# A list-scheduled attention kernel: where its transposes stand, and the paces its plan reckons with

## The chip, the cores and the metric

The kernel runs on one core of a Trainium2 chip. The metric is the device time of one execution in microseconds. Engine names are those of the profile: PE is TensorE (matmuls), PEld its weight loads, DVE VectorE, ACT ScalarE, POOL GpSimd, SP the engine whose queue issues all DMAs. A matmul multiplies a stationary operand, loaded beforehand by a weight load, with a moving operand that streams past it; its result lands in one of eight PSUM banks of 128 x 512 words.

## What is computed

Two attention layers A and B work on the same input and are mixed by a gate per token. Each layer has 32 heads of 20 features and goes through the 2048 tokens in 4 segments of 512: causal softmax attention inside the segment, and a memory `M`, `z` that sums earlier segments.

```python
def layer(x, wq, wk, wv, wo, beta):                 # 2048 x 640, H = 32, Dh = 20
    for s in range(4):                              # segments of 512 tokens
        p = softmax(qs @ ks.T * scale + mask)
        a_dot = p @ vs
        a_mem = (phi(qs) @ M) / (phi(qs) @ z + 1e-6)
        o = g * a_mem + (1 - g) * a_dot             # g = sigmoid(beta), per head
        M = M + phi(ks).T @ vs;  z = z + phi(ks).sum(tokens)
    return concat(o) @ wo
gate = sigmoid((x * gate_w).sum(-1))
return gate * layer_A + (1 - gate) * layer_B
...
phi(t) = t + 1 where t > 0, else exp(t)
```

## The kernel before

**Stages.** A step `t` (0 to 7) is one layer of one segment. Its projections q, k, v and o run in split precision: each operand is taken apart into a high and a low part, and three products are summed (`product`, matmuls of L695: 15 per 128 output features and half, with 512 or 320 columns). `qk_finish` and `hi_lo_out` split the results again and send them through DRAM into score operands (`qst`, `kst`), four heads at a time. Such a group of four heads is a slot `i`, 64 in all. A slot has S-units (`s_unit`, L1127: scores by query block, of which DVE takes the row maximum, L1114), a transpose of those maxima (`mrow_unit`, L1152), their copy into spare rows of `qst` by DMA, T-units (`t_unit`, L1217: scores by key block with the maximum already subtracted; ACT takes the exponential, L1209, POOL masks the diagonal, L1210), and one P·V group (`pv_unit`, L1237). `fin_unit` transposes the P·V result back and weighs it; `o_transpose` transposes the output for the o product; `back_unit` transposes phi(k) for the memory's update (`update_unit`, L883); `mem_unit` (L805) reads the memory. The last output products of the last step are full-array matmuls (L1056).

**Two halves.** Matmuls of 64 rows or fewer use one half of the array. The program keeps two sequences, `lane[0]` and `lane[1]`, and writes for each half its own matmuls; P·V and a few other groups use all 128 rows and join the halves (`whole`, `pv_unit`). A unit from `split_unit` has its lower-row part and its upper-row part; one half starts it (`firsts`), the other adds its own part later into the same bank (`seconds`). A transpose unit has four transposes for each half (`turn`, L843), the maxima's one.

**The order.** The whole program is laid out by a planner that runs when the kernel is built. It keeps a clock `clk`, plans when each instruction ends from given paces (`mm(n)` for a matmul of n columns, the numbers in `put(engine, duration, ...)`, `DONE` for signalling), and emits an instruction on an engine when the plan has it start. `op` and `next_start` reckon when a half can begin its next matmul: not before the one in front has streamed, and not before the weights are there, which can be fetched only once the one in front has begun (`lead`). Nothing of this runs on the chip; there the engines follow their own order and wait for each other by semaphores.

`lane_step` picks the next matmul of a half: first blocks of S- and T-units (`lane_ops`), then a second half that is ready, then the unit in progress; with none, `start_unit` starts a delayed unit (`start_late`, from the list `late` that `later` fills) or goes on with the projections (`fill`). Slots are spread over time by `marks`, and `RULES` gives each slot its order of S and T units and five numbers: `span`, `calm` (planned load of DVE above which low-priority delayed units are kept back), `lag` (time between the first half's last matmul and the second half's first), `room` and `hold`.

Of the kernel before, what the change touches and what calls it, by code (L numbers as in the profile page):

```python
# [15 lines left out]
AF = mybir.ActivationFunctionType  # L16
# [26 lines left out]
def tile_gated_mix_infini_attn(  # L43
# [50 lines left out]
        3: "TSTSTSTSTS 0.978 2.38 0.24 8 0.0",  # L94
        4: "TSTSTSTSTS 1.010 2.38 0.30 8 0.0",
        5: "TSSTTSSTTS 1.010 2.38 0.30 8 0.0",
        6: "TSTSTSTSTS 0.931 2.38 0.30 6 0.0",
        7: "TTSTSTSTSS 1.031 2.38 0.30 8 0.0",
        8: "TSTSTSTSTS 1.009 2.38 0.30 8 0.9",
        9: "STSTSTSTST 0.982 2.95 0.37 8 0.0",  # L100
        10: "TSTSTSTSTS 1.044 2.38 0.30 8 0.0",
        11: "TTSSTTSSTS 1.010 2.92 0.32 8 0.0",
        12: "TSTSTSTSTS 0.935 2.22 0.35 6 3.4",
        13: "TSTSTSTSTS 1.010 2.67 0.30 8 1.6",
        14: "TSTSTSTSTS 1.010 2.38 0.30 8 0.0",
        15: "TSTSTSTSTS 1.022 1.56 0.26 8 0.0",
        16: "TSTSTSTSTS 0.947 2.38 0.30 8 0.0",
        17: "TSTSTSTSTS 1.056 2.38 0.30 8 0.0",
        18: "TSTSTSTSTS 0.946 2.38 0.31 8 0.0",
        19: "TSTSTSTSTS 0.954 2.38 0.30 8 0.0",  # L110
        20: "STTSTSSTST 1.010 2.38 0.39 8 0.0",
        21: "TSTSTSTSTS 1.005 2.81 0.30 8 0.0",
        22: "TSTSTSTSTS 1.048 1.51 0.36 8 0.0",
        23: "TSSTTSSTTS 1.025 2.74 0.30 8 0.0",
        24: "TSTSTSTSTS 0.968 3.16 0.30 8 3.5",
        25: "TSTTSSTSTS 1.010 1.69 0.22 8 0.0",
        26: "TSTSTSTSTS 1.010 2.38 0.30 8 0.0",
        27: "TSTSTSTSTS 1.055 1.45 0.32 8 0.0",
        28: "TSTSTSTSTS 0.927 2.38 0.22 4 0.0",
        29: "TTSTSTSTSS 1.010 3.28 0.30 8 0.0",  # L120
        30: "TSTSTSTSTS 0.905 2.38 0.35 8 0.3",
        31: "TSTSTSTSTS 1.022 2.38 0.23 8 0.0",
        32: "TSTSTSTSTS 0.939 3.80 0.26 8 0.0",
        33: "TSTSTSTSTS 1.048 2.75 0.30 8 0.0",
        34: "TSTSTSTSTS 0.901 2.38 0.38 8 0.0",
        35: "TSTSTSTSTS 0.973 2.38 0.30 6 0.0",
        36: "STTSTSSTST 1.010 2.38 0.36 8 0.0",
# [1467 lines left out]
```

## Time and profile before

| | |
|---|---|
| median of 3 runs | 1045.03 us (1043.71 to 1046.25) |
| the profiled execution | 1042.96 us, span 1041.3 us |
| granted TensorE clock, mean | 0.999 |
| projections, L695, of the chain of waits | 52% |
| P·V, L1237 | 13% |
| T-units L1217, S-units L1127 | 7% each |
| transposes L843 | 4% |

The span runs from the first to the last instruction; the profiled execution's own time has 1.7 us more around it. A busy PE is not a PE at its peak: a matmul's recorded duration contains its way through the array, and any wait for its weights. So two matmuls are compared by the distance between their ends on the same half, and the two halves overlap in the timeline. A line of the timeline merges neighbours of one kind: it has the start of the first, the time from there to the end of the last, and the count.

### The profile page before, as it was taken

The page shows a single profiled execution, that of the slowest core. Times are in us where ns is not written, and L with a number is a line of the kernel's source. Part 1 is how long each engine was busy: PE and PEld are TensorE (multiplying, and loading weights), DVE is VectorE, ACT ScalarE, POOL GpSimd, SP SyncE. Part 2 cuts the span into 40 slices and gives each one's busy share as a digit, 9 for nine tenths or more (in the row PEclk, how much of TensorE's full clock was granted, in tenths as well). Part 3 has the DMA queues.
Part 4 walks back from the last instruction along what each step waited for, and adds up shares of the span by engine and source line. Part 5 has one row for each costly group of instructions (what it writes and reads, how often), then busy time and mean ns, then how long its engine had stood idle before and what let it go on. Part 6 is the DMA issues. An engine that isn't in the chain of part 4 may idle for free.

```text
span 1041.3 us, 31917 instructions
## 1 busy us (share of the span) xinstructions
PE 1031.3 (99%) x11780; PEld 870.4 (84%) x11780; DVE 760.8 (73%) x2725; ACT 660.2 (63%) x1337; POOL 581.7 (56%) x1043
## 2 busy tenths in 40 slices
PE   9999999999999999999999999999999999999998
PEld 7987888888888878888798887988879888888776
DVE  4787877558776688775877768976577767978844
ACT  5476666667564685665756557576574746757572
POOL 3565654556454674747736457375773635736462
PEclk9999999999999999999999999999999999999999
DMA  8997677658575486755858458674576855858432
GB/s 269 295 302 187 205 214 215 191 161 269 136 251 157 137 291 187 226 177 151 262 146 255 134 153 279 202 244 136 163 226 204 266 152 182 264 148 242 117 117 76
DMA packets 110028, 207.97 MB, mean 200 GB/s; under 512 B 12464, under 2 KB 16560, under 8 KB 109872
## 3 DMA queue, kind: packets, MB, share of 16 engines
q1 hardware_dynamic: 109872, 205.93, 65.2%
q8 instruction: 93, 1.52, 0.6%
q14 instruction: 63, 0.52, 0.2%
HBM read 131.43 MB, written 73.40 MB: 197 GB/s over the span
## 4 chain that ended last, share of the span: by engine, by line
PE 89%; DVE 3%; DMA 3%; ACT 2%; issue 1%; POOL 1%; SPq 0%; ACTq 0%; DVEq 0%; POOLq 0%
PE bank L695 52%; PE bank L1237 13%; PE bank L1217 7%; PE bank L1127 7%; PE bank L843 4%; PE bank L883 3%; PE bank L805 2%; DVE bank L1114 1%; DMA kd<-row 1%; DMA wst<-in_x_dram 1%; PE bank L741 1%; PE bank L1152 0%; POOL wl L524 0%; DMA row<-in_xT_dram 0%; PE bank L1056 0%
## 5 line engine op out<-in xcount | busy, mean ns | idle before, releaser
L1114 DVE CUSTOM_DVE_ANT_0 bank<-bank,tri 128x384 f32<-128x384 f32 (+3 forms) x1024 | 474.0, 522 | 146.3 <-PE bank L1127 117.6
L695 PE MATMUL bank<-row,wh 64*128 64x512 f32 x2308 | 535.2, 407 | 0.0
L1209 ACT ACTIVATE p<-bank 128x512 f32<-128x512 f32 x606 | 333.3, 599 | 155.6 <-PE bank L1217 124.5
L1210 POOL TENSOR_SCALAR_AFFINE_SELECT p<-p 128x256 f32<-128x256 f32 (+1 forms) x606 | 218.7, 370 | 243.9 <-ACT p L1209 233.4
L695 PEld LDWEIGHTS bank<-row,wh 64*128 64x128 f32 x2308 | 325.9, 185 | 12.4 <-issue 2.6
L695 PE MATMUL bank<-row,wl 64*128 64x512 f32 x1154 | 302.5, 402 | 0.0
L524 POOL TENSOR_TENSOR wl<-wst,wh 128x640 fp32r<-128x640 f32 x115 | 179.6, 1566 | 74.7 <-ACT wh L522 73.1
L695 PE MATMUL bank<-wvh,row 64*128 64x320 f32 x1280 | 202.4, 317 | 0.1
L1127 PE MATMUL bank<-kst,qst 60*128 60x384 f32 (+3 forms) x1024 | 176.9, 321 | 0.9 <-DVE O L1304 0.4
L695 PEld LDWEIGHTS bank<-row,wl 64*128 64x128 f32 x1154 | 170.4, 186 | 4.8 <-issue 0.6
L1217 PE MATMUL bank<-qst,kst 62*128 62x384 f32 (+3 forms) x1024 | 172.8, 323 | 1.1 <-DVE mw L819 0.7
L695 PEld LDWEIGHTS bank<-wvh,row 64*128 64x128 f32 x1280 | 161.1, 185 | 2.9 <-issue 1.4
L1237 PE MATMUL bank<-p,vst 128*32 128x128 f32 (+2 forms) x1980 | 148.3, 430 | 0.0
L1114 DVE DVE_READ_ACCUMULATOR2_ANT mx<- 128x1 f32 x1024 | 146.7, 143 | 0.0
L1217 PEld LDWEIGHTS bank<-qst,kst 62*128 62x128 f32 x1024 | 125.3, 185 | 17.1 <-DVE mx L1114 4.6
L1127 PEld LDWEIGHTS bank<-kst,qst 60*128 60x128 f32 x1024 | 125.1, 185 | 13.0 <-DVE mx L1114 2.9
L1237 PEld LDWEIGHTS bank<-p,vst 128*32 128x32 f32 x1980 | 59.4, 109 | 87.6 <-issue 68.3
L695 PE MATMUL bank<-wvl,row 64*128 64x320 f32 x640 | 113.3, 312 | 0.0
L522 ACT CAST wh<-wst 128x640 fp32r<-128x640 f32 x119 | 86.5, 736 | 34.5 <-PE bank L695 27.6
L695 PEld LDWEIGHTS bank<-wvl,row 64*128 64x128 f32 x640 | 88.7, 185 | 0.7 <-issue 0.4
L499 POOL TENSOR_TENSOR wvl<-wst,wvh 128x640 fp32r<-128x640 f32 (+1 forms) x48 | 63.9, 1336 | 21.3 <-ACT wvh L496 21.0
L664 DVE TENSOR_TENSOR row<-bank,row 128x512 fp32r<-128x512 f32 x80 | 54.4, 688 | 29.1 <-ACT row L652 15.3
(100 smaller groups left out, 1224.1 us busy)
## 6 DMA issues: line engine op xcount, KB each, us to landing
qd<-row SPq DMA_DIRECT2D x120, 256.0 KB
kd<-row SPq DMA_DIRECT2D x120, 256.0 KB
qst<-qd SPq DMA_DIRECT2D x128, 240.0 KB
kst<-kd SPq DMA_DIRECT2D x128, 240.0 KB
wst<-in_a_wq_dram SPq DMA_DIRECT2D x20, 320.0 KB
wst<-in_a_wk_dram SPq DMA_DIRECT2D x20, 320.0 KB
wst<-in_b_wq_dram SPq DMA_DIRECT2D x20, 320.0 KB
wst<-in_b_wk_dram SPq DMA_DIRECT2D x20, 320.0 KB
```

Of the source, the lines that this page charges most:

```text
L499: put("G", 0.77 * n, lambda: nc.gpsimd.tensor_tensor(out=wl[:, a:b, :], in0=w3, in1=r32(wh[:, a:b, :]), op=ALU.subtract), end, prio=4)
L522: put("A", 0.625, lambda: nc.scalar.copy(wh, w3), lambda: put(lo_eng, lo_cost, lambda: lo.tensor_tensor(out=wl, in0=w3, in1=r32(wh), op=AL ...
L524: lambda: lo.tensor_tensor(out=wl, in0=w3, in1=r32(wh), op=ALU.subtract), end, prio=3), prio=6)
L664: put("D", 0.605, lambda: nc.vector.tensor_tensor(out=lo, in0=src, in1=r32(hi), op=ALU.subtract), out, prio=1)
L695: return nc.tensor.matmul(bank_of, lhsT=w[ROWS[half]], rhs=x_[ROWS[half]], start=start, stop=stop)
L843: return nc.tensor.transpose(px[:, n, r], block(n)[r], ident[r, r])
L1114: put("D", w / 960.0 + 0.085, lambda: nc.vector.tensor_tensor_reduce(out=sc[:, off:off + w], in0=sc[:, off:off + w], in1=tri[:, L - w:], s ...
L1127: lane_ops[half].append((mm(w), lambda pair=pair, qb=qb, off=off, w=w, r=r, sc=sc: nc.tensor.matmul(sc[:, off:off + w], lhsT=q[r, pair, P ...
L1209: put("A", 0.483, lambda: nc.scalar.activation(pt, sc, AF.Exp, scale=SCALE), lambda: (bank.give(sc), put("G", 0.15 + 0.105 * len(todo), la ...
L1210: "G", 0.15 + 0.105 * len(todo), lambda: nc.gpsimd.affine_select(out=blocks, in_=blocks, pattern=[[0, len(todo)], [1, P]], base=0, channel ...
L1217: lane_ops[half].append((mm(w), lambda pair=pair, kb=kb, off=off, w=w, r=r, sc=sc: nc.tensor.matmul(sc[:, off:off + w], lhsT=k[r, pair, P ...
L1237: nc.tensor.matmul(po[32 * j:32 * j + 32, P * kb:], lhsT=vst[t % 2][:, kb, h * E1:h * E1 + 32], rhs=pts[i, n, f][0][:, off:off + w], start ...
```

## The change

- `RULES` has new entries for most slots and a sixth number, `wait`. Slots that have no entry keep the values of the slot in front.
- `mm(n)` counts 0.008 + 0.000438 n us where it counted 0.0004333 n. The two ACT reads of a projection's bank count 0.475 and 0.487 (0.483), the exponential behind the relu 0.525 (0.56). The row maximum counts 0.02 more, and what follows it is planned 0.05 later.
- In `hi_lo_phi`, the DVE operation `low_part` is planned only when both ACT operations that read the bank are through.
- `op` notes in `quick[half]` whether the matmul just placed is shorter than the load of the next weights; P·V sets it for both halves.
- Delayed units that are transposes carry the time at which they were asked for (`later(..., turns=True)`); memory and update units do not. `start_late` takes a transpose unit only once it is `wait` old. With `only=True` it takes transpose units at once, whatever their age. `lane_step` asks so right behind a quick matmul, also inside a product in progress, and `start_unit` does when nothing else is there.
- A transpose unit that one half has begun is finished without a break; the second half's part is taken when the second half has a quick matmul behind it, or `wait` later.

```diff
@@ -88,79 +88,74 @@
     RULES = {
-        0: "TTSTSTSTSS 1.055 2.80 0.30 8 0.0",
-        1: "TSSTTSSTTS 1.010 2.38 0.33 4 0.0",
-        2: "STTSTSSTST 1.010 1.93 0.39 8 0.0",
...
+        0: "TSTSTSTSTS 0.906 2.61 0.29 8 0.0 1.6",
+        1: "STSTSTSTST 1.025 2.27 0.25 8 0.0 1.6",
+        2: "TSTSTSTSTS 1.060 2.14 0.30 8 0.0 0.29",
...
     }
     rule = {}
     DONE = {"A": 0.17, "D": 0.135, "G": 0.11, "S": 0.0}
     FULL, LEADT = 0.113, 0.056
     def mm(n):
-        return 0.008 + n * 0.0004333, FULL, 1
+        return 0.008 + n * 0.000438, FULL, 1
     def quad4(n):
         return 0.0027 + n / 1200.0, FULL, 2
@@ -239,6 +234,7 @@
     begun = [0.0, 0.0]
     fetched = [0.0]
     joined = [True]
+    quick = [True, True]
     def whole(dur, emit):
         if not joined[0]:
@@ -269,6 +265,7 @@
         for _ in range(parts - 1):
             start += max(stream, 0.003 + lead)
         begun[half], lane[half] = start, start + stream
+        quick[half] = lead + 0.003 > stream
         advance(now[0])
         return emit()
@@ -622,8 +619,8 @@
     late = []
-    def later(prio, cost, ok, fn):
-        late.append((prio, next(seq), cost, ok, fn))
+    def later(prio, cost, ok, fn, turns=True):
+        late.append((prio, next(seq), clk[0] if turns else None, ok, fn))
         late.sort(key=lambda x: x[:2])
@@ -648,19 +645,19 @@
                     "D", 0.605, lambda: nc.vector.tensor_tensor(out=r32(y), in0=pp, in1=r32(y), op=ALU.min), end, prio=1), prio=1)
             read = then_all(2, over)
-            hi_lo_out(pp, hi, lo, dst, m, read, then)
-            put("A", 0.483, lambda: nc.scalar.activation(r32(y), pp, AF.Exp), read, prio=1)
+            low = hi_lo_out(pp, hi, lo, dst, m, read, then, 2)
+            put("A", 0.487, lambda: nc.scalar.activation(r32(y), pp, AF.Exp), lambda: (low(), read()), prio=1)
         else:
             both = then_all(2, lambda: put("D", 0.605, lambda: nc.vector.scalar_tensor_tensor(
                 out=r32(y), in0=pp, scalar=0.0, in1=r32(y), op0=ALU.max, op1=ALU.add), end, prio=1))
-            hi_lo_out(pp, hi, lo, dst, m, both, then)
-            put("A", 0.483, lambda: nc.scalar.activation(r32(y), pp, AF.Relu, scale=-1.0), lambda: put(
-                "A", 0.56, lambda: nc.scalar.activation(r32(y), r32(y), AF.Exp, scale=-1.0), both, prio=1), prio=1)
-
-    def hi_lo_out(src, hi, lo, dst, m, read, then):
+            low = hi_lo_out(pp, hi, lo, dst, m, both, then, 2)
+            put("A", 0.487, lambda: nc.scalar.activation(r32(y), pp, AF.Relu, scale=-1.0), lambda: (low(), put(
+                "A", 0.525, lambda: nc.scalar.activation(r32(y), r32(y), AF.Exp, scale=-1.0), both, prio=1)), prio=1)
+
+    def hi_lo_out(src, hi, lo, dst, m, read, then, reads=1):
         is_q = any(dst is x for x in qd)
-        def low():
+        def low_part():
             put("D", 0.605, lambda: nc.vector.tensor_tensor(out=lo, in0=src, in1=r32(hi), op=ALU.subtract), out, prio=1)
         def out():
@@ -677,7 +674,9 @@
                     dma(0.7, lambda c=c, part_=part_: nc.sync.dma_start(
                         out=r32(dst[P * m:P * (m + 1), c, :]), in_=r32(part_)), one, prio=-1)
-        put("A", 0.483, lambda: nc.scalar.copy(hi, src), low, prio=1)
+        low = then_all(reads, low_part)
+        put("A", 0.475, lambda: nc.scalar.copy(hi, src), low, prio=1)
+        return low
     def hold_on(cond, what=""):
         while not cond():
@@ -687,7 +686,7 @@
     blocked = [""]
     def split_unit(lower, upper, done, credit=0.0):
-        return dict(ops=(deque(lower), deque(upper)), n=(len(lower), len(upper)), done=done, credit=credit)
+        return dict(turn=lower[0][0] is TURN, ops=(deque(lower), deque(upper)), n=(len(lower), len(upper)), done=done, credit=credit)
     def product(bank_of, terms, step, done):
         def run(half, n, start, stop):
@@ -780,7 +779,7 @@
                 mem_asked.add((t, h))
                 for n in range(NB):
                     later(4, 0.75, lambda: Ot[t] is not None and t in gq and all(
-                        (t - 2, mm) in upd_done for mm in mem_tiles(h)), lambda n=n, h=h: mem_unit(t, n, h))
+                        (t - 2, mm) in upd_done for mm in mem_tiles(h)), lambda n=n, h=h: mem_unit(t, n, h), False)
     def mem_unit(t, n, h):
         mbd = mbds[t % 2]
@@ -854,7 +853,7 @@
         def got(pkn):
             def end():
                 bank.give(b)
-                later(3, 1.0, lambda: ok(), lambda: update_unit(t, m, pkn))
+                later(3, 1.0, lambda: ok(), lambda: update_unit(t, m, pkn), False)
             either(0.483, lambda: nc.scalar.copy(r32(pkn), b), 0.605, lambda: nc.vector.tensor_copy(r32(pkn), b), end, 3)
@@ -1111,11 +1110,11 @@
                 read = then_all(len(todo), end)
                 def one(pair, qb, off, then):
                     w = P * (qb + 1)
-                    put("D", w / 960.0 + 0.085, lambda: nc.vector.tensor_tensor_reduce(
+                    put("D", w / 960.0 + 0.105, lambda: nc.vector.tensor_tensor_reduce(
                         out=sc[:, off:off + w], in0=sc[:, off:off + w], in1=tri[:, L - w:],
                         scale=1.0, scalar=LOWEST, op0=ALU.add, op1=ALU.max,
                         accum_out=mx[i][:, half, pair, qb:qb + 1],
-                    ), then, prio=3)
+                    ), lambda: at(clk[0] + 0.05, then), prio=3)
                 if len(todo) > 1:
                     one(*todo[0], lambda: (one(*todo[1], read), read()))
@@ -1244,6 +1243,7 @@
         now[0] += 0.11
         lane[:] = begun[:] = [now[0], now[0]]
         fetched[0] = now[0]
+        quick[:] = [True, True]
         def read():
             for n in range(5):
@@ -1374,69 +1374,89 @@
     filled = [0.0]
     over = [False]
-    def start_late(keep, upto=9):
+    def start_late(half, upto=9, only=False):
         for x in late:
-            prio, _, cost, ok, fn = x
+            prio, _, born, ok, fn = x
             if prio > upto:
                 return None
-            if len(bank.free) <= (0 if prio <= 0 else keep) or (prio > 2 and load["D"] > rule["calm"]):
+            if only and born is None or not only and born is not None and clk[0] - born < rule["wait"]:
+                continue
+            if not bank.free or (prio > 2 and load["D"] > rule["calm"]):
                 continue
             if ok():
                 late.remove(x)
                 return fn()
-    def start_unit(half):
-
-        u = start_late(0)
+    def start_unit(half, any_=False):
+
+        u = start_late(half)
         if u is None and not over[0]:
             u = next(fill, -1.0)
             if u == -1.0:
                 over[0] = True
                 u = None
+        if u is None:
+            u = start_late(half, only=True)
         if isinstance(u, dict):
             firsts[half].append(u)
             return True
         filled[0] += u or 0.0
         return bool(u)
+    def run_second(half, u):
+        if u["ins"]:
+            after_ins(u["ins"])
+            u["ins"] = None
+        form, emit = u["ops"][half].popleft()
+        op(half, form, lambda: emit(False, not u["ops"][half]))
+        filled[0] += u["credit"]
+        if not u["ops"][half]:
+            seconds[half].remove(u)
+            at(lane[half] + 0.2, u["done"])
+        return True
+
+    def run_first(half, u):
+        form, emit = u["ops"][half].popleft()
+        u["ins"] = op(half, form, lambda: emit(len(u["ops"][half]) + 1 == u["n"][half], False))
+        filled[0] += u["credit"]
+        if not u["ops"][half]:
+            firsts[half].remove(u)
+            u["at"] = lane[half] + rule["lag"]
+            (seconds[1 - half].append if u["credit"] else seconds[1 - half].appendleft)(u)
+        return True
+
     def lane_step(half):
+        begun_ = [u for u in seconds[half] if u["turn"] and len(u["ops"][half]) < u["n"][half]]
+        if begun_:
+            return run_second(half, begun_[0])
+        if firsts[half] and firsts[half][-1]["turn"]:
+            return run_first(half, firsts[half][-1])
+        if quick[half]:
+            for u in seconds[half]:
+                if u["turn"] and max(now[0], lane[half], begun[half] + 0.003 + LEADT) >= u["at"]:
+                    return run_second(half, u)
+            u = start_late(half, only=True)
+            if u:
+                firsts[half].append(u)
+                return run_first(half, u)
         if lane_ops[half]:
-            dur, emit, end = lane_ops[half].popleft()
-            op(half, dur, emit)
+            form, emit, end = lane_ops[half].popleft()
+            op(half, form, emit)
             if end:
                 at(lane[half] + 0.2, end)
             return True
         u = seconds[half][0] if seconds[half] else None
-        if u and next_start(half, u["ops"][half][0][0][1])[1] >= u["at"]:
-            if u["ins"]:
-                after_ins(u["ins"])
-                u["ins"] = None
-            dur, emit = u["ops"][half].popleft()
-            op(half, dur, lambda: emit(False, not u["ops"][half]))
-            filled[0] += u["credit"]
-            if not u["ops"][half]:
-                seconds[half].popleft()
-                at(lane[half] + 0.2, u["done"])
-            return True
+        if u and next_start(half, u["ops"][half][0][0][1])[1] >= u["at"] + (rule["wait"] if u["turn"] else 0.0):
+            return run_second(half, u)
         if not firsts[half]:
-            if u and u["at"] - max(now[0], lane[half]) < 0.02:
+            if u and u["at"] - max(now[0], lane[half]) < 0.02 and not u["turn"]:
                 return False
             if not start_unit(half):
+                if u and u["turn"] and next_start(half, LEADT)[1] >= u["at"]:
+                    return run_second(half, u)
                 return False
-
-        if len(firsts[half]) == 1 and firsts[half][0]["credit"] and len(firsts[half][0]["ops"][half]) > 2:
-            u = start_late(0, 0)
-            if u:
-                firsts[half].append(u)
-        u = firsts[half][-1] if firsts[half] else None
-        if u:
-            dur, emit = u["ops"][half].popleft()
-            u["ins"] = op(half, dur, lambda: emit(len(u["ops"][half]) + 1 == u["n"][half], False))
-            filled[0] += u["credit"]
-            if not u["ops"][half]:
-                firsts[half].pop()
-                u["at"] = lane[half] + rule["lag"]
-                (seconds[1 - half].append if u["credit"] else seconds[1 - half].appendleft)(u)
+        if firsts[half]:
+            run_first(half, firsts[half][-1])
         return True
     pv_due = deque()
@@ -1494,7 +1514,7 @@
     def rules(i):
         if i in RULES:
-            order, rule["span"], rule["calm"], rule["lag"], rule["room"], rule["hold"] = RULES[i].split()
+            order, rule["span"], rule["calm"], rule["lag"], rule["room"], rule["hold"], rule["wait"] = RULES[i].split()
             rule.update({x: float(rule[x]) for x in rule if x != "order"}, order=order)
```

More of the change, by code (lines that the diff above doesn't have):

```diff
@@ L102, in tile_gated_mix_infini_attn @@
[L102 to L112, printed above, removed]
```

52 lines of the change are left out of this document (removed), and 58 rows, old and new, of the table RULES.

## The prediction

> **What bounds the kernel now.** I read the page first: the span, the busy shares, the clock and the chain of waits.
>
> ```profile
> span 1041.3 us, 31917 instructions
> PE 1031.3 (99%) x11780; PEld 870.4 (84%) x11780; DVE 760.8 (73%) x2725; ACT 660.2 (63%) x1337; POOL 581.7 (56%) x1043
> ...
> PEclk9999999999999999999999999999999999999999
> ...
> PE 89%; DVE 3%; DMA 3%; ACT 2%; issue 1%; POOL 1%; SPq 0%; ACTq 0%; DVEq 0%; POOLq 0%
> ```
>
> TensorE is busy 99% of the span at full clock, it carries 89% of the chain, and the next engine (DVE) is at 73%. So a microsecond is gained only where TensorE's own sequence gets shorter, or where it stops less often. The table by stage says that no single stage matters:
>
> ```profile
> 0.00:60.00 60.00, 57.55 (x516) 50.88 (x518) 37.01 (x118) 32.49 (x63) 29.90 (x46) 1.00 0.90 281
> 60.00:1023.00 963.00, 960.56 (x11172) 809.16 (x11174) 716.27 (x2595) 625.93 (x1271) 551.77 (x998) 1.00 0.65 197
> 1023.00:1037.00 14.00, 13.22 (x103) 10.37 (x92) 7.51 (x13) 1.76 (x3) 0.00 (x0) 1.00 0.14 47
> ```
>
> The columns after the length are busy times of PE, PEld, DVE, ACT and POOL. From 60 to 1023 us PE leaves 2.4 us uncovered, while PEld (the weight loads) leaves 154. Busy PE hides how close together the matmuls stand, so the spacing has to be read from the timeline. The two halves of the array (rows 0 to 63 and 64 to 127) run side by side, each in its own order; the pace that counts is that of one half.
>
> **What a transpose costs, by what stands in front of it.** I take ends (start plus duration), because a matmul that waits for its weights is recorded as begun and merely longer. Plain 512-column products on one half:
>
> ```profile
> 121.55 0.39 PE L695 MATMUL bank<-row,wh 64*128 64x512 f32 x1
> ...
> 121.78 0.39 PE L695 MATMUL bank<-row,wh 64*128 64x512 f32 x1
> ```
>
> That is one every 0.23 us. Four transposes between two of them, on one half:
>
> ```profile
> 276.88 0.50 PE L695 MATMUL bank<-row,wh 64*128 64x512 f32 x1
> ...
> 277.22 0.34 PE L843 MATMUL bank<-ident,row 64*128 64x64 f32 x3
> ...
> 277.40 0.22 PE L843 MATMUL bank<-ident,row 64*128 64x64 f32 x1
> 277.43 0.48 PE L695 MATMUL bank<-row,wh 64*128 64x512 f32 x1
> ```
>
> The product in front ends at 277.38, the one behind at 277.91: 0.53, less 0.23 for the product itself, is 0.30 us for four transposes. The first three span 0.34, so their ends are (0.34 - 0.22)/2 = 0.06 apart, and the product behind ran 0.48 in place of 0.39. That is the extra: its weights could only begin to load when the last transpose began, and a transpose is too short to hide them.
>
> A 128-column matmul is too short as well. First one with a product behind it, then one with four transposes in between:
>
> ```profile
> 167.16 0.22 PE L1217 MATMUL bank<-qst,kst 62*128 62x128 f32 x1
> ...
> 167.22 0.44 PE L695 MATMUL bank<-row,wh 64*128 64x512 f32 x1
> ```
>
> ```profile
> 462.56 0.22 PE L1127 MATMUL bank<-kst,qst 60*128 60x128 f32 x1
> 462.62 0.28 PE L843 MATMUL bank<-ident,O 64*128 64x64 f32 x2
> ...
> 462.75 0.28 PE L843 MATMUL bank<-ident,O 64*128 64x64 f32 x2
> 462.84 0.47 PE L695 MATMUL bank<-row,wh 64*128 64x512 f32 x1
> ```
>
> Without transposes it is 167.66 - 167.38 = 0.28, of which 0.05 (0.28 - 0.23) is the unhidden load. With them it is 463.31 - 462.78 = 0.53. So the four cost 0.25 us here: the 0.05 was already paid. Behind the last matmul of a P·V group (L1237) the same holds, shown with a 320-column product behind:
>
> ```profile
> 515.14 0.62 PE L1237 MATMUL bank<-p,vst 128*32 128x256 f32 x12
> ...
> 515.69 0.41 PE L695 MATMUL bank<-wvh,row 64*128 64x320 f32 x1
> ```
>
> ```profile
> 696.80 0.40 PE L1237 MATMUL bank<-p,vst 128*32 128x128 f32 x8
> ...
> 697.13 0.27 PE L843 MATMUL bank<-ident,O 64*128 64x64 f32 x1
> 697.17 0.39 PE L695 MATMUL bank<-wvh,row 64*128 64x320 f32 x1
> 697.25 0.34 PE L843 MATMUL bank<-ident,O 64*128 64x64 f32 x3
> ```
>
> Plain, from 515.76 to 516.10: 0.34. With four transposes the last of them ends at 697.59; the 320-column matmul behind it adds about 0.20 (0.15 of its own, 0.05 load), which makes 697.79 - 697.20 - 0.34 = 0.25. So a run of transposes is worth 0.05 us more behind a long matmul than behind a short one or a P·V group, and breaking a run in two costs 0.05 again.
>
> **The change part by part.** *Where the runs stand.* The transposes are the same in number: 1072 of L843 and 128 of L1152.
>
> ```profile
> L843 PE MATMUL bank<-ident,row 64*128 64x64 f32 x752 | 74.5, 225 | 0.0
> ...
> L843 PE MATMUL bank<-ident,O 64*128 64x64 f32 x320 | 35.8, 225 | 0.1
> ...
> L1152 PE MATMUL bank<-ident,mt 64*32 64x64 f32 x128 | 27.9, 218 | 0.0
> ```
>
> In the instruction orders of the two programs I counted, on each half, the runs of transposes with nothing else of that half between, and what precedes each. Before: 348 runs, of which 252 behind a long matmul (over 128 columns), 33 behind a 128-column one, 37 behind P·V, 26 behind memory and update matmuls. After: 336 runs, of which 105 long, 118 short, 76 P·V, the other 37 mostly memory and update matmuls. So 147 runs leave the long matmuls and 12 breaks go: 159 × 0.05 = 8.0 us over two halves, 4.0 us on one. Pricing every neighbouring pair of both orders with the median interval that this trace shows for that pair gives 4.9 us less on one half, but 3.3 less when the halves must meet at every P·V group. I take 3.9, with 3.3 and 4.9 as ends.
>
> *Recalibrated paces* (matmul, the two reads of the bank, the score maximum): they run nothing faster; they move orders only. The maximum (L1114) now counts 0.02 us longer and its bank comes free 0.05 us later in the plan, so a score matmul that takes that bank is planned later. What it could save is what score matmuls now wait for that bank:
>
> ```profile
> PEld bank L1217 <- DVE mx L1114: 4.6, 20, 0.5
> ...
> PEld bank L1127 <- DVE mx L1114: 2.9, 12, 0.5
> ```
>
> At best 7.5 us, in 32 waits of 0.23 on average. But measured by the pace of TensorE, the distance in the order between two uses of such a bank hardly grows (lower quartile 1.98 us before and 1.86 after behind a single maximum, 2.23 and 2.21 behind two): the new order uses up what the later release gives. Nor is a loss excluded. Ends -7.5 and +3; I take -0.9, near nothing, because the distances are the direct evidence.
>
> *`low` waits for both ACT reads of the bank.* In the plan that delays the split's low part by one ACT operation. On the chip it is waiting already, with DVE standing still in front of it:
>
> ```profile
> DVE row L664 <- ACT row L652: 15.3, 20, 1.9
> ...
> DVE row L664 <- ACT row L657: 8.7, 8, 5.6
> ```
>
> 24.0 us of DVE in 28 waits. In the new order DVE takes score maxima meanwhile, and banks come free sooner. The TensorE loads released by the end of that chain (L648) bound the gain:
>
> ```profile
> PEld bank L1217 <- DVE row L648: 2.4, 8, 0.4
> ...
> PEld bank L1127 <- DVE row L648: 0.9, 3, 0.4
> ```
>
> Between 0 and -3.3; I take -1.2, since some of these waits only change their name. The low part's three copies to DRAM on SP's queue start no later than now.
>
> *Held-back transposes.* They wait up to 1.6 us of planned time (0.03 to 2.46 in the table) for a short matmul. Queued behind them are the maxima's rows for the T-blocks, the updates, the attention output's transposes. The tightest is the first: its copy into the score operand must land before the slot's first T-block. By paces, that distance is at least 4.2 us before and 4.1 after, median 12.8 and 11.9: cost 0. Cover gone, it would delay TensorE directly. At the end, the transposes of the last output tile have seven full-array products (L1056) left behind them, not fifteen:
>
> ```profile
> 1028.29 0.92 PE L843 MATMUL bank<-ident,O 64*128 64x64 f32 x8
> ...
> 1029.24 0.59 ACT L1332 CAST row<-bank 128x512 fp32r<-128x512 f32 x1 [3.95 <-PE bank L843]
> ...
> 1029.87 0.69 DVE L1332 TENSOR_TENSOR row<-bank,row 128x512 fp32r<-128x512 f32 x1
> ```
>
> From the last transpose (1029.21) to the split's end (1030.56) are 1.35 us; seven products at 0.23 are 1.6. It still fits: cost 0, and 0.2 to 0.5 if it does not.
>
> A rule speaks against this pricing. The Trainium skill, "TensorE: Matmul & The Clock Gate", section "LDWEIGHTS (loading the stationary operand)", gives the load time by columns alone, columns/1.2 ns, 107 ns for 128. Transposes load 128 columns, so by it they would stand 0.107 apart anywhere; a run of four would cost an estimated 0.46 behind a long matmul and 0.43 behind a short one, and the 147 moved runs would give about 2.1 us on a half in place of 3.7. The trace does not agree for transposes: their ends stand 0.06 apart above.
>
> **Sum.** -3.9 - 0.9 - 1.2 = -6.0. Against the profiled execution: span 1041.3 - 6.0 = 1035.3, plus the 1.7 around it (1042.96 - 1041.3) is 1037.0. That execution was 2.1 below the median of the three runs, 1045.03; the forecast for a median is 1039.0.
>
> **The rivals.** (1) *The stalls go too.* All idle of the weight loads ahead of score and T-block matmuls:
>
> ```profile
> L1217 PEld LDWEIGHTS bank<-qst,kst 62*128 62x128 f32 x1024 | 125.3, 185 | 17.1 <-DVE mx L1114 4.6
> ...
> L1127 PEld LDWEIGHTS bank<-kst,qst 60*128 60x128 f32 x1024 | 125.1, 185 | 13.0 <-DVE mx L1114 2.9
> ```
>
> 30.1 us over both halves, about 15 on one. If the truer plan removes half of that, 7.5 more than the pace gain: 1045.0 - 3.9 - 7.5 = 1033.6. Against it stand the unchanged bank distances. (2) *The gain is handed back.* A shorter TensorE sequence reaches the same eight banks earlier, DVE and ACT are no faster, and each microsecond saved returns as a wait ahead of L1217 and L1127: 1045, at most 1 lower. For it: the bank distance behind T-blocks shrinks a little too (lower quartile 1.44 to 1.40 for single pieces). Against it: DVE is idle 27%. (3) *Slower.* Transposes now enter between the two halves of a product, which keeps that product's bank longer, and of eight banks one fewer is free for score blocks. Price: one more wait of 0.23 (7.5/32) per slot in half of the 64 slots is 7.4, less 3.9: 1048.5. It decides from 17 extra waits on (3.9/0.23). Against it: the bank distances above shrink by 0.02 to 0.12 at the lower quartile, less than such a wait. (4) *It does not do what it says*: the new table could have undone the placement. The counted runs rule that out.
>
> **How the numbers follow.** The forecast 0.50, own range 1035 to 1043; rival 1 0.22; rival 2 0.15; rival 3 0.13; rival 4 none. Time 1039. The bounds (-4.9 - 7.5 - 3.3 = -15.7 and -3.3 + 3 = -0.3) and the rivals reach from 1029 to 1048.5; the far ends are unlikely together, so the range is 1030 to 1047, which leaves out most of rival 3. About 0.2% (2.1 us) is what a measurement of this kernel tells from no change. Faster takes rival 1 and nearly all of the forecast, 0.71; within, rival 2 and a remainder, 0.16; slower, 0.13.
>
> **What would show it.** Right: four transposes cost 0.25 behind 128-column blocks in the timeline of after; idle of PEld before L1217 and L1127 stays within 25 to 32 us; the waits of L664 on L652 and L657 fall well below 24. Wrong: that idle grows beyond 38 (rival 3), or falls below 22 (rival 1), or the product behind a transpose run still takes 0.05 more than when it stands behind a short matmul.

## The result and the profile after

The changed kernel takes 1028.43 us (median of 4, 1028.07 to 1028.68), the kernel before 1044.37 us (median of 4 in the same session). The ratio is 0.9847, 95% interval 0.9828 to 0.9865: 16 us faster, where 6 were forecast, and below the stated range. In the changed kernel most line numbers are a few lower: transposes are L842, S-units L1126, T-units L1216, row maxima L1113, P·V L1236, products L694.

The page of the changed kernel, in the order of the one before:

```profile
span 1026.3 us, 31848 instructions
PE 1017.5 (99%) x11780; PEld 869.6 (85%) x11780; DVE 758.1 (74%) x2719; ACT 662.5 (65%) x1343; POOL 582.5 (57%) x1043
...
PEclk9999999999999999999999999999999999999999
```

The work is the same: 11780 matmuls, weight loads busy 869.6 us (870.4 before), DVE 758.1 (760.8). The span is 15.0 shorter and busy PE falls by 13.8 with the same matmuls, which shows that waiting for weights stands inside "busy PE". TensorE still bounds the kernel.

The placement is what the prediction said. The timeline of the changed kernel, one half, a 128-column block, four transposes and a product:

```profile
891.15 0.22 PE L1126 MATMUL bank<-kst,qst 60*128 60x128 f32 x1
891.21 0.22 PE L842 MATMUL bank<-ident,O 64*128 64x64 f32 x1
...
891.27 0.28 PE L842 MATMUL bank<-ident,O 64*128 64x64 f32 x2
...
891.39 0.22 PE L842 MATMUL bank<-ident,O 64*128 64x64 f32 x1
891.43 0.47 PE L694 MATMUL bank<-row,wh 64*128 64x512 f32 x1
```

From 891.37 to 891.90 is 0.53, less the 0.28 that block and product need without transposes: 0.25 for the four.

The stops are not what it said. Weight loads ahead of score blocks, from the groups of instructions (the last figure group is the idle time of the weight-load queue in front of them):

```profile
L1126 PEld LDWEIGHTS bank<-kst,qst 60*128 60x128 f32 x1024 | 128.1, 185 | 11.5 <-issue 1.2
L1216 PEld LDWEIGHTS bank<-qst,kst 62*128 62x128 f32 x1024 | 127.9, 186 | 7.5 <-DVE ft L1304 0.8
```

19.0 us, against 13.0 + 17.1 = 30.1 before: less than the 22 that the prediction named as the sign of its rival 1. The releasers say which stops went, from the table of waits, which lists stops of 0.15 us and more (total, number, longest):

```profile
PEld bank L1126 <- DVE mx L1113: 0.8, 4, 0.2
...
PEld bank L1216 <- DVE mx L1113: 0.4, 2, 0.2
```

At score blocks, waits for the row maxima's banks fell from 32 (7.5 us) to 6 (1.2 us). Those on the last operation of the low part's chain (L648 before, L645 now), 11 with 3.3 us before, have left the table. These two are 9.6 of the 11.1; the stops too short for the table add up to 12 us both before and after. DVE's own standstill in front of the low part went from 24.0 to 16.8 us:

```profile
DVE row L661 <- ACT row L654: 10.0, 8, 5.6
...
DVE row L661 <- ACT row L649: 6.8, 7, 2.6
```

And the end, where the transposes of the last output tile now have seven full-array products behind them:

```profile
1015.62 0.98 PE L842 MATMUL bank<-ident,O 64*128 64x64 f32 x8
...
1017.26 0.69 DVE L1332 TENSOR_TENSOR row<-bank,row 128x512 fp32r<-128x512 f32 x1 [1.87 <-ACT row L1332]
...
1018.25 0.39 PE L1055 MATMUL bank<-row,wh 128*128 128x512 f32 x1
1018.48 0.39 PE L1055 MATMUL bank<-row,wl 128*128 128x512 f32 x1
```

The split ends at 1017.95, and the products run on at 0.23: the cover held.

**A sum that closes.** On one half, from its first matmul's end to its last, the trace of before has 1034.0 us, that of after 1019.5. Pricing every neighbouring pair of matmuls with the median interval of its kind over the traces gives, as the mean of the halves, 994.7 before and 991.4 after. So the placement shortened the pace by 3.3 us, and what exceeds the pace fell from 39.3 to 28.1, by 11.2, on both halves alike. Idle of the weight-load queue ahead of score blocks fell by 11.1. The experiments ask what removed these stops.

### The profile page after: what moved, and what is told of

Read it like the earlier page. It is cut to its first block, busy times and chain, and to the rows that moved or that the text cites. A ratio compares the mean times of both kernels' runs of the same rounds, so it can differ in the third digit from the quotient of the medians.

```text
span 1026.3 us, 31848 instructions
## 1 busy us (share of the span) xinstructions
PE 1017.5 (99%) x11780; PEld 869.6 (85%) x11780; DVE 758.1 (74%) x2719; ACT 662.5 (65%) x1343; POOL 582.5 (57%) x1043
## 4 chain that ended last, share of the span: by engine, by line
PE 60%; DMA 1%; ACT 0%; DVE 0%; POOL 0%; issue 0%; SPq 0%; ACTq 0%
PE bank L694 34%; PE bank L1236 9%; PE bank L1216 5%; PE bank L1126 4%; PE bank L842 3%; PE bank L804 2%; PE bank L882 1%; PE bank L1151 1%; DMA wst<-in_a_wv_dram 1%; DMA wst<-in_a_wq_dram 0%; PE bank L1055 0%; DVE row L1040 0%; DMA kd<-row 0%; POOL wl L521 0%; ACT p L1208 0%
## 5 line engine op out<-in xcount | busy, mean ns | idle before, releaser
L1113 DVE CUSTOM_DVE_ANT_0 bank<-bank,tri 128x256 f32<-128x256 f32 (+3 forms) x1024 | 475.3, 519 | 146.3 <-PE bank L1126 111.9
L694 PE MATMUL bank<-row,wh 64*128 64x512 f32 x2308 | 534.0, 405 | 0.0
L1208 ACT ACTIVATE p<-bank 128x512 f32<-128x512 f32 x596 | 327.4, 599 | 153.7 <-PE bank L1216 116.3
L694 PEld LDWEIGHTS bank<-row,wh 64*128 64x128 f32 x2308 | 328.8, 186 | 10.0 <-issue 0.6
L694 PE MATMUL bank<-row,wl 64*128 64x512 f32 x1154 | 313.0, 400 | 0.0
L694 PE MATMUL bank<-wvh,row 64*128 64x320 f32 x1280 | 201.0, 315 | 0.0
L694 PEld LDWEIGHTS bank<-row,wl 64*128 64x128 f32 x1154 | 180.6, 186 | 5.2 <-issue 0.4
L1126 PE MATMUL bank<-kst,qst 60*128 60x384 f32 (+3 forms) x1024 | 180.0, 321 | 1.3 <-issue 0.4
L1216 PE MATMUL bank<-qst,kst 62*128 62x128 f32 (+3 forms) x1024 | 177.5, 320 | 0.0
L694 PEld LDWEIGHTS bank<-wvh,row 64*128 64x128 f32 x1280 | 162.4, 185 | 1.1 <-DVE row L661 0.2
L1236 PE MATMUL bank<-p,vst 128*32 128x384 f32 (+3 forms) x1952 | 148.2, 429 | 0.0
L1113 DVE DVE_READ_ACCUMULATOR2_ANT mx<- 128x1 f32 x1024 | 144.1, 141 | 0.0
L1126 PEld LDWEIGHTS bank<-kst,qst 60*128 60x128 f32 x1024 | 128.1, 185 | 11.5 <-issue 1.2
L1216 PEld LDWEIGHTS bank<-qst,kst 62*128 62x128 f32 x1024 | 127.9, 186 | 7.5 <-DVE ft L1304 0.8
L1236 PEld LDWEIGHTS bank<-p,vst 128*32 128x32 f32 x1952 | 59.3, 110 | 86.8 <-issue 64.0
L694 PE MATMUL bank<-wvl,row 64*128 64x320 f32 x640 | 112.4, 312 | 0.0
L694 PEld LDWEIGHTS bank<-wvl,row 64*128 64x128 f32 x640 | 88.6, 185 | 0.3
L1263 ACT COPY row<-bank 128x512 f32<-128x512 f32 x57 | 33.6, 589 | 62.8 <-PE bank L1236 59.4
```

Source lines behind the costliest of these rows:

```text
L694: return nc.tensor.matmul(bank_of, lhsT=w[ROWS[half]], rhs=x_[ROWS[half]], start=start, stop=stop)
L1113: put("D", w / 960.0 + 0.105, lambda: nc.vector.tensor_tensor_reduce(out=sc[:, off:off + w], in0=sc[:, off:off + w], in1=tri[:, L - w:], s ...
L1126: lane_ops[half].append((mm(w), lambda pair=pair, qb=qb, off=off, w=w, r=r, sc=sc: nc.tensor.matmul(sc[:, off:off + w], lhsT=q[r, pair, P ...
L1208: put("A", 0.483, lambda: nc.scalar.activation(pt, sc, AF.Exp, scale=SCALE), lambda: (bank.give(sc), put("G", 0.15 + 0.105 * len(todo), la ...
L1216: lane_ops[half].append((mm(w), lambda pair=pair, kb=kb, off=off, w=w, r=r, sc=sc: nc.tensor.matmul(sc[:, off:off + w], lhsT=k[r, pair, P ...
L1236: nc.tensor.matmul(po[32 * j:32 * j + 32, P * kb:], lhsT=vst[t % 2][:, kb, h * E1:h * E1 + 32], rhs=pts[i, n, f][0][:, off:off + w], start ...
```

## The experiments

One quantity is needed to read them. The planner has a clock, and its plan of a kernel ends at some time on it: 1014.2 for the kernel before, 1016.1 for the changed one. That is no measurement. But measured time minus planned end, the gap, tells how far the chip departs from the plan: 30.2 before, 12.3 after. Of this, 7.2 is only the matmul's pace: the new one counts 0.0000047 us more per column, and one half streams 1740 × 512 columns of products, 960 × 320, and 256 × 1280 of scores. Where a kernel has the old matmul pace, the last column below has that 7.2 taken off. "Unfitted" in the column of tables means a table that was made for another plan; "fitted" means one made for this kernel's plan. "Idle ahead of S and T" is the idle time of the weight-load queue ahead of score blocks.

| kernel | table | planned end | measured | gap | idle ahead of S and T | gap, same matmul pace |
|---|---|---|---|---|---|---|
| before | its own | 1014.2 | 1044.4 | 30.2 | 30.1 | 23.0 |
| after | its own | 1016.1 | 1028.4 | 12.3 | 19.0 | 12.3 |
| table_only | new, old plan | 1037.4 | 1073.4 | 36.0 | 34.9 | 28.8 |
| place_only | unfitted | 1039.3 | 1079.9 | 40.6 | 38.8 | 33.4 |
| max_only | unfitted | 1046.0 | 1071.4 | 25.4 | 26.4 | 18.2 |
| low_only | unfitted | 1040.8 | 1069.0 | 28.2 | 27.7 | 21.0 |
| paces_only | unfitted | 1045.8 | 1059.1 | 13.3 | 21.3 | 13.3 |
| after_oldmax | unfitted | 1046.8 | 1076.7 | 29.9 | 33.6 | 29.9 |
| after_oldlow | unfitted | 1053.0 | 1077.5 | 24.5 | 30.5 | 24.5 |
| place_fit | fitted | 1018.0 | 1050.0 | 32.0 | 28.2 | 24.8 |
| paces_fit | fitted | 1025.6 | 1041.8 | 16.2 | 24.6 | 16.2 |
| oldmax_fit | fitted | 1026.2 | 1052.7 | 26.5 | 30.2 | 26.5 |
| after_fit | fitted | 1015.5 | 1029.9 | 14.4 | 21.9 | 14.4 |
| tbank_fit | fitted | 1020.0 | 1036.1 | 16.1 | 23.5 | 16.1 |

**One part at a time, table untouched.** The kernel before with all new paces; then the new placement with old paces and the old table; then the new table alone; and the changed kernel with the maximum's old pace.

```diff
paces_only: before, with
-        return 0.008 + n * 0.0004333, FULL, 1
+        return 0.008 + n * 0.000438, FULL, 1
-                    put("D", w / 960.0 + 0.085, ...
-                    ), then, prio=3)
+                    put("D", w / 960.0 + 0.105, ...
+                    ), lambda: at(clk[0] + 0.05, then), prio=3)
+            (and the changed kernel's hi_lo_phi and hi_lo_out)
```

> The kernel before with the new paces (matmul, bank reads, row maximum, order of the low part), old placement of transposes and old table. Theory A (the missing 10 us came from the paces: banks behind row maxima are planned free later, so score matmuls no longer stop for them): about 1033 to 1037, idle of the weight loads ahead of S- and T-units falls from 30 to about 20 us. Theory B (it came from the placement or the table): 1042 to 1047, that idle stays near 30.

```diff
place_only: after, with the three edits of paces_only undone, and
-        0: "TSTSTSTSTS 0.906 2.61 0.29 8 0.0 1.6",
+        0: "TTSTSTSTSS 1.055 2.80 0.30 8 0.0 1.6",
...
```

> The new placement of transposes with old paces and the old table (wait 1.6 in every slot). Priced gain of the placement alone 3.5 to 4: Theory A expects 1039 to 1042 with idle ahead of S- and T-units near 30 us. Theory B, if placement removes the stalls too: 1030 to 1035.

```diff
table_only: before, with
-        0: "TTSTSTSTSS 1.055 2.80 0.30 8 0.0",
+        0: "TSTSTSTSTS 0.906 2.61 0.29 8 0.0",
...
```

> The kernel before with the new table alone (its sixth number dropped). Theory A: the table fits another plan, so it does nothing for the better here: 1043 to 1055. Theory B, if the table itself chooses orders that stop less: 1033 to 1038.

```diff
after_oldmax: after, with
-                    put("D", w / 960.0 + 0.105, ...
-                    ), lambda: at(clk[0] + 0.05, then), prio=3)
+                    put("D", w / 960.0 + 0.085, ...
+                    ), then, prio=3)
```

> The changed kernel with only the row maximum's old pace (0.02 shorter, bank free 0.05 earlier in the plan). Theory A: the stalls behind two-part score banks return, 1034 to 1039, idle ahead of S- and T-units back to 26 to 30 us. Theory B: 1027 to 1031, idle near 19.

Measured: 1059.1, 1079.9, 1073.4 and 1076.7 us, ratios to before 1.015 [1.0135, 1.0165], 1.0349 [1.0331, 1.0366], 1.0284 [1.0269, 1.0300] and 1.0317 [1.0302, 1.0333]. Each part alone is slower than either whole. All four times lie above what theory A gave, and the reason is one that neither theory had: a table is fitted to one plan. A constant that changes by 0.02 us moves every later decision, the orders differ from the first slots on, and the plan itself grows by 23 to 32 us.

The idle of the weight loads, however, moved the way theory A had it for the two kernels that take the paces or leave one out; with the new placement alone it is 38.8, where theory A had it stay near 30. Groups of instructions of paces_only (all new paces, old placement), then of after_oldmax:

```profile
L1129 PEld LDWEIGHTS bank<-kst,qst 60*128 60x128 f32 x1024 | 126.7, 185 | 10.7 <-issue 2.1
L1219 PEld LDWEIGHTS bank<-qst,kst 62*128 62x128 f32 x1024 | 125.8, 185 | 10.6 <-DVE mx L1116 1.8
```

```profile
L1126 PEld LDWEIGHTS bank<-kst,qst 60*128 60x128 f32 x1024 | 124.7, 185 | 20.4 <-DVE mx L1113 6.5
L1216 PEld LDWEIGHTS bank<-qst,kst 62*128 62x128 f32 x1024 | 125.2, 185 | 13.2 <-DVE mx L1113 2.9
```

21.3 us with the paces and without the placement (about 20 forecast); 33.6 with the placement and without the one pace (26 to 30 forecast).

**Which pace.** The maximum alone on the kernel before, the low part's order alone, and the low part's order undone in the changed kernel. The last two move the ACT paces of the bank reads as well; no run separates them from the order.

```diff
max_only: before, with
-                    put("D", w / 960.0 + 0.085, ...
-                    ), then, prio=3)
+                    put("D", w / 960.0 + 0.105, ...
+                    ), lambda: at(clk[0] + 0.05, then), prio=3)
```

> The kernel before with only the row maximum's new pace. Its plan ends at 1046.0 on the planner's own clock (before 1014.2, after 1016.1); measured minus planned was 30 to 42 in every kernel with the old maximum and 12 to 13 in the two with the new one. Theory A (the maximum's pace closes that gap): gap 13 to 20, so 1059 to 1066, and idle of the weight loads ahead of S- and T-units 19 to 23 us. Theory B (another of the new paces closes it): gap 30 or more, 1076 and up, idle 30 or more.

```diff
low_only: before, with
-        put("A", 0.483, lambda: nc.scalar.copy(hi, src), low, prio=1)
+        low = then_all(reads, low_part)
+        put("A", 0.475, lambda: nc.scalar.copy(hi, src), low, prio=1)
+        return low
+            (and the changed kernel's hi_lo_phi)
```

> The kernel before with only the new order of the low part and its ACT paces; its plan ends at 1040.8. Theory A: the gap stays above 27, 1068 to 1080, idle ahead of S- and T-units 28 to 38 us. Theory B (DVE no longer standing in front of the low part is what helps): gap below 20, 1053 to 1061.

```diff
after_oldlow: after, with
-        low = then_all(reads, low_part)
-        put("A", 0.475, lambda: nc.scalar.copy(hi, src), low, prio=1)
-        return low
+        put("A", 0.483, lambda: nc.scalar.copy(hi, src), low, prio=1)
+            (and the old hi_lo_phi)
```

> The changed kernel with the old order of the low part and its old ACT paces; its plan ends at 1053.0. Theory A: gap 12 to 20, 1065 to 1073, idle ahead of S- and T-units 19 to 24 us. Theory B: gap 25 or more, 1078 and up, and DVE waits of the low part on the second ACT read grow above 20 us.

Measured 1071.4 (1.0259 [1.0244, 1.0275]), 1069.0 (1.0233 [1.0214, 1.0252]) and 1077.5 (1.0324 [1.0301, 1.0347]). Theory A as stated falls: the maximum alone leaves a gap of 25.4, not 13 to 20, and with only the low part's order undone the gap is 24.5, not 12 to 20. Nor does theory B hold as stated for the maximum (a gap of 30 or more) or for the low part alone (below 20; it is 28.2, as theory A had it); with the low part's order undone the figures stop just short of its 25 and 1078. Adding either alone closes only a little of the gap (25.4 and 28.2, from 30.2), undoing either opens more than all of it (29.9 and 24.5, from 12.3); but the tables of these kernels are unfitted, so neither is the pace's own price.

The table of waits tells the maximum's part without the plan: stops behind the maxima's banks at score blocks number 6 to 21 in the seven kernels with its new pace (11 in max_only, 9 in paces_only) and 19 to 46 in the seven without (32 before, 38 in after_oldmax). That the low part's order does what it was read to do is in the DVE waits of after_oldlow, 26.2 us where the changed kernel has 16.8:

```profile
DVE row L661 <- ACT row L649: 13.9, 18, 3.1
...
DVE row L661 <- ACT row L654: 12.3, 14, 5.6
```

One of these waits cost far more than its own length, and it inflates this kernel's gap. DVE stood 3.06 us in front of the low part, TensorE stood 3.50 us until the bank behind it was free, and from 445 to 460 us the granted clock (the third figure from the end of the last line) was 0.66 on average:

```profile
446.95 0.69 DVE L661 TENSOR_TENSOR row<-bank,row 128x512 fp32r<-128x512 f32 x1 [3.06 <-ACT row L649]
...
449.09 1.37 PE L802 MATMUL bank<-mbd,row 64*128 64x84 f32 x9 [3.50 <-DVE row L645]
```

```profile
445.00:460.00 15.00, 11.50 (x102) 11.32 (x102) 7.07 (x20) 3.72 (x7) 4.90 (x6) 0.66 0.41 139
```

From 444 to 462 us each half falls 8 to 10 us behind its pace. That is most of the 12.2 by which undoing the low part's order opened the gap: an example of what that order prevents, and no measure of what it is worth throughout.

**With tables fitted to each plan.** To compare like with like, tables were searched anew for three partial kernels and for the changed one, by changing entries of single slots and keeping what ended the plan earlier. Nothing but the table differs from the kernel named in each expectation.

```diff
place_fit, paces_fit, oldmax_fit, after_fit: place_only, paces_only, after_oldmax, after, with
-    RULES = {...}
+    RULES = {...}    (fitted to that kernel's plan)
```

> New placement and old paces as in place_only, with a table fitted to that plan (the planner's own end falls from 1039.3 to 1018.0). Theory A (placement is worth only its 3 to 4 us, and old paces leave a gap of 30 to 40 between plan and chip): 1048 to 1058, idle of the weight loads ahead of S- and T-units 30 us or more. Theory B (a fitted table with the new placement is the gain): 1028 to 1036.

> Old placement and all new paces as in paces_only, with a table fitted to that plan (planned end from 1045.8 to 1025.6). Theory A: gap 12 to 14, 1037 to 1040, faster than before although its plan is 11 longer; idle ahead of S- and T-units 18 to 22 us. Theory B: 1050 or more.

> The changed kernel with only the row maximum's old pace, as after_oldmax, with a table fitted to that plan (planned end from 1046.8 to 1026.2). Theory A (the maximum's pace alone opens the gap by some 17): 1050 to 1058, idle ahead of S- and T-units 28 to 36 us. Theory B (an untuned order, not the pace, cost after_oldmax its gap): 1036 to 1042, idle 18 to 24.

> The changed kernel with its table fitted a little further (planned end 1015.5 for 1016.1). Gap 12: 1027 to 1029, no difference that can be told from the changed kernel; a scatter of orders alone shows as 1024 to 1032.

Measured 1050.0 (1.0056 [1.0041, 1.0071]), 1041.8 (0.9980 [0.9968, 0.9991]), 1052.7 (1.0077 [1.0061, 1.0094]) and 1029.9 (0.9862 [0.9847, 0.9877]). The two kernels with the new placement but without the maximum's pace stay slower than before; by the last column their gaps, 24.8 and 26.5, are like the 23.0 of before, as theory A had it. The one with all paces and the old placement is 2.6 faster than before, although its plan, without the 7.2, is 4.2 longer; it missed every figure of theory A (1037 to 1040, a gap of 12 to 14, idle of 18 to 22), if only by a few us. after_fit, with a plan 0.6 shorter than the changed kernel's, came out 1.4 slower: just outside the 1027 to 1029 expected, and within the 1024 to 1032 that a scatter of orders was given.

Over all kernels one division stands out. The five with all the new paces (after, paces_only, paces_fit, after_fit, tbank_fit) have 19.0 to 24.6 us of idle ahead of score blocks and 12.3 to 16.2 in the last column; the nine others have 26.4 to 38.8 and 18.2 to 33.4. Neither the placement nor the table divides them so: table_only has the new table and 34.9 us of idle.

**The same correction at another bank.** After the change, the bank that a T-unit's exponential reads (L1208) is among the causes named most often for the stops left, with 1.3 of the 19.0 us, so that release was made later too.

```diff
tbank_fit: after, with
-                put("A", 0.483, lambda: nc.scalar.activation(pt, sc, AF.Exp, scale=SCALE), lambda: (bank.give(sc), put(
+                put("A", 0.483, lambda: nc.scalar.activation(pt, sc, AF.Exp, scale=SCALE), lambda: (at(clk[0] + 0.08, lambda: bank.give(sc)), put(
+            (and RULES fitted to it)
```

> The changed kernel with one pace more made longer in the same way: the bank that the exponential of a T-unit reads is planned free 0.08 later; table fitted to that plan (planned end 1020.0, against 1016.1 of the changed kernel). Theory A (too early a release in the plan is what stops TensorE, whichever reader): idle of the weight loads ahead of S- and T-units falls from 19 to 14 to 17 us and the gap from 12 to 7 to 10, so 1027 to 1030. Theory B (only the maxima's banks mattered): idle stays at 19 or more, gap 12 or more, 1032 to 1036.

1036.1 us (0.9922 [0.9907, 0.9937]). Idle is 23.5 us and the gap 16.1; theory A is wrong here, and B holds but for a time 0.1 above its range:

```profile
L1131 PEld LDWEIGHTS bank<-kst,qst 60*128 60x128 f32 x1024 | 127.4, 185 | 14.2 <-DVE mx L1118 3.2
L1221 PEld LDWEIGHTS bank<-qst,kst 62*128 62x128 f32 x1024 | 131.1, 185 | 9.3 <-DVE mx L1118 0.7
```

The waits behind the maxima came back a little (3.9 us in these two rows, 1.2 after). Making a release later in the plan does not help at every bank. None of these kernels is faster than the changed one.

## Why the prediction was wrong

**Placement: right in the pace.** The forecast took -3.9, with ends -3.3 and -4.9. The pace sum of the two orders is 3.3 shorter, and in the kernels with the new placement it lies between 990.2 and 992.4 us, in those with the old between 994.7 and 996.0. It does not show in the time of a kernel with old paces: place_fit is slower than before. Transposes stand 0.06 apart in the changed kernel as well.

**Recalibrated paces: the step that failed.** The sum took -0.9 for the maximum and -1.2 for the low part, 2.1 in all; on each half the excess over the pace fell by about 11. The bounds that the prediction set beside these two terms, 7.5 and 3.3, were nearly used up: stops behind the maxima fell by 6.3, those behind the end of the low part's chain by 3.3. So the stops were named rightly and sized wrongly. Two readings led to it.

First, the distances between two uses of a bank. They hardly change, as stated, and were taken as the direct evidence that the stops would stay. The stops went all the same, from 32 to 6 behind the maxima. The reading that fits is that what counts is whether the distance is longer than what DVE needs at that point, which depends on what stands ahead in DVE's queue; the planner reckons with that, and with the new paces it reckons better. No run tests this by itself.

Second, the price of idle, which set rival 1. It took the 30.1 us of idle weight loads as "about 15 on one" half, as if each half stood still for its own stops alone. But the column counts time in which no load of either half is under way. One stop in the trace of before, matmuls first and then the weight loads:

```profile
150.24 0.40 PE L695 MATMUL bank<-row,wl 64*128 64x512 f32 x1
150.32 0.40 PE L695 MATMUL bank<-row,wh 64*128 64x512 f32 x1
151.15 0.50 PE L1127 MATMUL bank<-kst,qst 60*128 60x256 f32 x4 [0.43 <-DVE O L1304]
```

```profile
151.15 0.30 PEld L1127 LDWEIGHTS bank<-kst,qst 60*128 60x128 f32 x4 [0.87 <-DVE O L1304]
151.37 0.31 PEld L695 LDWEIGHTS bank<-row,wh 64*128 64x128 f32 x3
```

The two products, one on each half, end at 150.64 and 150.72; then neither half has a matmul until the late load at 151.15. The eight longest stops of this kind (over 0.4 us, 4.4 together) put one half 3.8 and the other 4.4 behind its pace. Shorter ones are partly covered: over the traces of before and after, a microsecond of this idle puts each half back by about 0.7 (a straight line through stretches of 10 us), where halving has 0.5. By that, the 11.1 that went are some 8 of the 11; where the other 3 went is not located. Among the 14 kernels, gap and idle rise together about one to one (12.3 and 19.0, 23.0 and 30.1, 33.4 and 38.8), but their tables differ too. The reading that fits is that both halves are fed by one weight-load queue. The Trainium skill, "TensorE: Matmul & The Clock Gate", section "Step-by-step: what each phase is for", has the matmuls of one TensorE in program order, with only weight loads pulled ahead; by that rule a load that waits for its bank ends up stopping whatever follows it, on either half, and the stop shown agrees. At 0.7, rival 1's "half of that" would have been 10.5, and its time 1030.6.

**The low part.** Its effect was rightly named (DVE standing in front of it), and its bound of 3.3 was met by the loads that the chain's last operation releases. Whether DVE's queue passes more of the delay on, to the maxima behind it, is not shown: after_oldlow has 21 stops behind maxima where the changed kernel has 6, but its table is unfitted.

**The table** was read as numbers without a price. It weighs most: the seven kernels whose table was made for another plan are 15 to 36 us slower than before.

**Held-back transposes and the end: right as far as seen**, both at cost 0. The products at the end ran on without a gap, and the table of waits names no DMA as what a weight load waited for, so none for the maxima's rows; no run isolates the holding back.

The sum as measured: 3.3 from the pace of the order and 11.2 from the stops is 14.5 on the halves, as in the two profiled executions (1034.0 to 1019.5); the other 0.5 of the span's 15.0 is at its ends. The last 1.0 of the medians' 16 is that the profiled execution of before was faster than its median.

**Open.** How much of the 11 belongs to the maximum and how much to the low part: the waits speak for 6.3 and 3.3, but no pair of fitted kernels differs in one of them alone except after_fit and oldmax_fit, where the maximum's pace goes with 12.1 of gap and 8.3 of idle; kernels with all the new paces scatter by 4 in gap. What placement is worth in a fitted kernel: paces_fit to after is 13.4, but the first one's plan is fitted less far. And where the kernels with unfitted tables lose the rest: in after_oldmax the excess over pace is 75.8 with 33.6 of idle ahead of score blocks, 42 more, where before and after have 9 more. Some of it is in the plan itself, some in stretches of lower clock like the one shown (mean clock 0.994 in after_oldlow, 0.997 in place_only); at which operations was not followed.

## What to carry to other kernels

Idle time of a queue that feeds two parallel halves stops both; here each half lost about 0.7 of it, so do not divide it by the halves. When a change makes a plan truer, price it by the stops that it could remove, and ask for more than unchanged distances before calling them safe. In a kernel whose order is planned, compare the plan's end with the measured time: a wide gap can say that a pace in the plan is wrong. And a part of such a change, tried without fitting the schedule again, tells little by its time; read the waits as well.

## What was not expected of the hardware

A pace that is 0.02 us too short and a release 0.05 us too early, with an order that put DVE in front of a blocked operation, went with about 11 us of 1044. In the trace of before, a load that waited for a maximum started about 0.05 us after the maximum's last instruction ended (52 or 53 ns in 31 of the 32 stops), so the stop itself is almost all the maximum's lateness. The mean of those stops was 0.23 us, several times the error of the plan.

And one late bank can cost far more than its own delay: in after_oldlow a stop of 3.5 us stands in a stretch of 15 us whose granted clock is 0.66, and each half lost 8 to 10 us there.
